# Bucketed attention and a SiLU MLP: another order of Silu and combinations in the last batch's rounds, other buffers for its larger chunk's outputs

## The chip, the cores and the metric

The kernel runs on one core of a Trainium2 chip. Times are device microseconds of one execution, from the median of three runs; the profile is one execution recorded by the hardware profiler, and its span (297.0 us) is a little shorter than the device time of the same run. The engines are named as in the profile: PE multiplies matrices, ACT (ScalarE) evaluates functions and copies, DVE (VectorE) and POOL (GpSimd) do elementwise work, SP issues transfers. Each takes its instructions in a fixed order, and an instruction that waits holds up those behind it.

## The reference, cut to what matters

Four batches of eight heads with 768 tokens and 64 features go through attention in which a query sees only the keys of its own hash bucket (the signs of six projections). The heads of a batch are put side by side into a matrix x of 768 tokens by 512 features, and x goes through two matrices with a SiLU between them:

```
h = x @ w_in                     # (3072 x 512) @ (512 x 2048)
g = h * (1 / (1 + exp(-h)))      # SiLU
out = g @ w_out                  # (3072 x 2048) @ (2048 x 512)
```

The change concerns the second part alone, and of it the last batch.

## The kernel before, in words

For most of the time attention and the MLP run interleaved: while heads of one batch go through attention, the MLP of the batch before fills PE's free places from a list of units. When attention has ended, the last batch's MLP is left, together with some units of the batch before. That is `tail`, from about 248 us of the profile on.

**Seven products instead of eight.** `tail` cuts both matrix products into 2 x 2 blocks and uses the Strassen-Winograd scheme: seven block products (numbered 1 to 7), with sums and differences of blocks before and after. In the first product the two halves of the tokens (384 each) are the rows, so four blocks of h come out: (0,0), (0,1), (1,0) and (1,1), as `gb(r, c, k)` names their SiLU values, k being one of eight blocks of 128 hidden features. `t_comb` forms the differences of x on DVE; those of w_in were made earlier on POOL.

**Rounds.** A loop takes two feature blocks a round: f = 0, 2, 4, 6. For each feature block `prod(n, f)` issues two matmuls of 384 columns (line 689). Products 1, 6, 5 and 3 accumulate one after the other in the same bank of PSUM (`bank[1, f]`, three banks in turn, tag "s"), and after each of the first three ACT copies the running sum out (`copy`, line 699, into `part[1]`, `part[6]`, `part[5]`). So product 6 of a block has to wait for the copy after product 1, product 5 for the copy after product 6, product 3 for the copy after product 5, and product 1 of the block three further on for the Silu that empties the bank. Product 2 has a bank of its own; products 7 and 4 share one (three banks in turn for both, tag "m"). DVE adds these to the copied sums (`add`, line 702): product 2 to part 1, product 7 to part 5, product 4 to part 6. Product 4 of a round is done in the next round (`old`).

**Silu.** A block is finished by Silu on ACT (`silu`, line 705): of part 1 for (0,0), straight from the bank after product 3 for (1,0), of part 5 for (1,1), of part 6 for (0,1). The Silus of parts 5 and 6 take two feature blocks in one instruction (128 x 768); the others take one (128 x 384). Part 5 is ready once product 7 is added; part 6 only in the next round. In the kernel before, the Silu of part 5 stands at the end of its round on ACT, and that of part 6 in the next round, after the copies of product 6.

**Combinations.** The second product needs differences of the Silu values: `combs(f)` makes (1,0)+(1,1) and, from it, s2 on DVE (lines 714 and 716) and s3 on POOL (line 718); `comb4(f)` makes s4 on POOL (line 724). They belong to the round before the one in which they are issued, and stand in DVE's queue ahead of that round's sums of product 2.

**Filler.** `filler` issues one unit of the batch before (eight matmuls of 256 columns, and for some a sum and an output transfer, lines 542 to 553). Rounds f = 0, 2 and 4 have one ahead of product 2, round 6 has none there and one at its end.

**The last product.** `last(ci, n, t)` multiplies the Silu values by w_out, again in seven products, in two chunks of the token blocks: chunk 0 has two blocks of 128 tokens (called the larger one here), chunk 1 one. A loop runs them alternately: 1, -1, 6, -2, 2, -6, 5, -5, 7, 3, -3, -7, 4, -4, a minus sign marking the smaller chunk. A product is 8 matmuls of 256 columns for each token block (line 800). Products 1, 2 share a bank, as do 6, 5, 3 and 7, 4, so -4 has to wait until -7 has been read out. Results of 1, 6 and 5 are kept; those of 2, 3, 7 and 4 are outputs. They are written into a buffer `osb` (line 810 on ACT for product 2, line 812 on DVE for the others) and sent by SP (line 819). All eight outputs take turns in three buffers of one pool, `ops`. The pool `thp` holds three buffers of the same size (128 x 512 in 4 bytes); the rounds keep part 1 in them, and after the rounds nobody does.

Order on each engine is the order of the calls in the code; nothing reorders it.

Of the kernel before, what the change touches and what calls it, by code (L numbers as in the profile page):

```python
# [9 lines left out]
F32 = mybir.dt.float32  # L10
# [7 lines left out]
def kernel(  # L18
# [15 lines left out]
    P = 128  # L34
# [20 lines left out]
    thp = ctx.enter_context(tc.tile_pool(name="thp", bufs=3))  # L55
# [112 lines left out]
    NK = NFT // 2  # L168
    NC = DMODEL // 2
# [286 lines left out]
    def flush():  # L456
        for fn in after:
            fn()
        after.clear()
# [189 lines left out]
    def tail(fill):  # L649
# [16 lines left out]
        def gb(r, c, k, n=1):  # L666
            t = G[2 * (2 * r + c) + k // 4]
            return t[:, k % 4 * NR0 : (k % 4 + n) * NR0]
# [5 lines left out]
        bank, part = {}, {}  # L674

        def prod(n, f):
            i = {1: 1, 6: 1, 5: 1, 3: 1, 2: 2, 7: 3, 4: 3}[n]
            first = n in (1, 2, 7)
            if first:
                bank[i, f] = ps.tile([P, NR0], F32, tag="s" if i == 1 else "m", name="h_ps", bufs=3)  # L680
            for dt in range(2):
                fs = slice(f * P, (f + 1) * P)
                f2 = slice(NF + f * P, NF + (f + 1) * P)
                w, x = {1: (w_in16[:, dt, fs], xb(0, r0, dt)),
                        2: (w_in16[:, 2 + dt, fs], xb(1, r0, dt)),
                        4: (w_in16[:, 2 + dt, f2], T[4][:, dt]),
                        3: (sw[4, dt][:, fs], xb(1, r1, dt))}.get(n) or \
                    (sw[{5: 1, 6: 2, 7: 3}[n], dt][:, fs], T[{5: 1, 6: 2, 7: 3}[n]][:, dt])
                nc.tensor.matmul(bank[i, f], w, x, start=(first and dt == 0), stop=True,  # L689
                                 skip_group_check=True)  # L690

        def copy(n, f):
            if n == 1:
                part[1, f] = thp.tile([P, NR0], F32, tag="th", name="part1")
            elif f % 2 == 0:
                t = ld.tile([P, 2, NR0], F32, tag="ldq" if n == 6 else "ldk", name=f"part{n}")
                part[n, f], part[n, f + 1] = t[:, 0], t[:, 1]
                part[n, "both", f] = t
            nc.scalar.copy(out=part[n, f], in_=bank[1, f])  # L699

        def add(n, i, f):
            nc.vector.tensor_tensor(out=part[n, f], in0=bank[i, f], in1=part[n, f], op=ALU.add)

        def silu(dst, x):
            nc.scalar.activation(out=dst, in_=x, func=AF.Silu)  # L705

        def both(n, f):
            return part[n, "both", f].rearrange("p f c -> p (f c)")

        def combs(f):  # L710
            w = slice(f, f + 2)
            f16 = lambda t: t[:, w].rearrange("p f c -> p (f c)")
            s3[f // 2] = xpl.tile([P, 2 * NR0], F16, tag="xpr", name="gs3", bufs=4)
            nc.vector.tensor_tensor(out=gb(1, 0, f, 2), in0=gb(1, 0, f, 2), in1=gb(1, 1, f, 2),
                                    op=ALU.add)
            nc.vector.tensor_tensor(out=f16(s2), in0=gb(1, 0, f, 2), in1=gb(0, 0, f, 2),
                                    op=ALU.subtract)
            nc.gpsimd.tensor_tensor(out=s3[f // 2], in0=gb(1, 1, f, 2), in1=f16(s2),  # L718
                                    op=ALU.subtract)

        def comb4(f):
            w = slice(f, f + 2)
            f16 = lambda t: t[:, w].rearrange("p f c -> p (f c)")
            nc.gpsimd.tensor_tensor(out=f16(s4), in0=gb(0, 1, f, 2), in1=f16(s2),
                                    op=ALU.subtract)

        def filler(n=1):
            for _ in range(n):
                if fill:
                    fill.popleft()()  # L730
                    flush()

        def old(a):
            for f in (a, a + 1):
                prod(4, f)
                add(6, 3, f)
# [6 lines left out]
        for f in range(0, NK, 2):  # L743
            fs = (f, f + 1)
            for g in fs:
                prod(1, g)
                copy(1, g)
            if f == 0:
                filler(2)
            else:  # L750
                old(f - 2)
            for g in fs:
                prod(6, g)
                copy(6, g)
            if f:
                silu(gb(0, 1, f - 2, 2), both(6, f - 2))
                combs(f - 2)
                comb4(f - 2)
            if f < NK - 2:
                filler()  # L760
            for g in fs:
                prod(2, g)
                add(1, 2, g)
            for g in fs:
                prod(5, g)
                copy(5, g)
            for g in fs:
                prod(7, g)
                add(5, 3, g)
                silu(gb(0, 0, g), part[1, g])  # L770
            for g in fs:
                prod(3, g)
                silu(gb(1, 0, g), bank[1, g])
            silu(gb(1, 1, f, 2), both(5, f))
            if f in (0, NK - 2):
                filler()
        old(NK - 2)
        filler(len(fill))
        combs(NK - 2)
# [5 lines left out]
        def last(ci, n, t):  # L785

            nt, t0 = ((2, 0), (1, 2))[ci]
            i, x, y = {1: (1, (0, 0), B11), 2: (1, (0, 1), B21),
                       6: (2, 2, wt[2]), 5: (2, (1, 0), wt[1]), 3: (2, 4, B22),
                       7: (3, 3, B12), 4: (3, (1, 1), wt[4])}[n]  # L790
            first = t == 0 and n in (1, 6, 7)
            if first:
                bank["o", ci, i] = ps.tile([P, nt, NC], F32, tag="ms"[ci], name="o2_ps", bufs=3)
            op = bank["o", ci, i]
            cs = slice((t0 + t) * P, (t0 + t + 1) * P)
            for k in range(NK):
                a = {2: s2[:, k], 4: s4[:, k],
                     3: s3[k // 2][:, k % 2 * NR0 : (k % 2 + 1) * NR0]}[x] \
                    if isinstance(x, int) else gb(x[0], x[1], k)
                nc.tensor.matmul(op[:, t, :], a[:, cs], y[:, k],  # L800
                                 start=(first and k == 0), stop=True, skip_group_check=True)
            if t < nt - 1:
                return
            with_part = {1: None, 2: None, 6: 1, 5: 1, 3: 1, 7: 5, 4: 6}[n]
            keep = n in (1, 6, 5)
            pool = nrm if keep else ops
            o = pool.tile([P, nt, NC], F32, tag=f"part{ci}{n}" if keep else "osb", name="osb",
                          bufs=1 if keep else 3)
            if with_part is None:
                nc.scalar.copy(out=o, in_=op)  # L810
            else:
                nc.vector.tensor_tensor(out=o, in0=op, in1=kept[ci, with_part], op=ALU.add)
            if keep:
                kept[ci, n] = o
                return
            r, c = {2: (0, 0), 3: (0, 1), 7: (1, 1), 4: (1, 0)}[n]
            dst = out[b * S : (b + 1) * S, c * NC : (c + 1) * NC].rearrange(
                "(p t) n -> p t n", p=P)
            nc.sync.dma_start(out=dst[:, 3 * r + t0 : 3 * r + t0 + nt, :], in_=o)

        for n in (1, -1, 6, -2, 2, -6, 5, -5, 7, 3, -3, -7, 4, -4):
            for t in range(2 if n > 0 else 1):
                last(int(n < 0), abs(n), t)
# [112 lines left out]
    for w in range(NW):  # L936
# [8 lines left out]
        keep = 3 if w >= NW - 12 else 0  # L945
        left = BST - w % BST
        n = -(-(len(moeq) - keep) // left) if len(moeq) > keep else 0
# [5 lines left out]
        if n == 1 and len(moeq) - keep < left and skip:  # L953
            n = 0
# [13 lines left out]
    act = nrm.tile([P, 1], F32, tag="act", name="act", bufs=1)  # L968
    nc.scalar.activation(out=act, in_=sc[:, 0:1], func=AF.Silu)
    tail(late)  # L970
# [1 line left out]
_INS = ['q', 'k', 'v', 'proj', 'moe_w_in', 'moe_w_out']  # L972
# [26 lines left out]
```

The softmax here doesn't subtract the row's maximum and nothing guards it: scores larger than these inputs give would overflow.

## Time and profile before

Time before: 298.57 us, the median of three runs from 298.52 to 298.67. Granted clock of PE in the profile: 1.00.

| | PE | ACT | DVE | POOL |
|---|---|---|---|---|
| busy, whole span of 297.0 us | 288.7 us (97%) | 224.6 us (76%) | 200.5 us (68%) | 202.9 us (68%) |
| busy, 255.64 to 261.12 us (round f = 2) | 5.48 | 4.66 | 4.44 | 2.02 |
| busy, 261.12 to 267.48 us (round f = 4) | 5.80 | 5.54 | 4.49 | 3.74 |
| busy, 267.48 to 273.83 us (round f = 6) | 5.80 | 6.16 | 4.32 | 3.22 |
| busy, 273.83 to 290.20 us (last product) | 16.37 | 3.78 | 6.42 | 3.98 |

The stretches are cut where product 1 of a round starts on PE. An engine's busy time counts only its own instructions, not waits. Matmuls are pipelined and their ends modelled, so a matmul's recorded end lies after the next one's start; a PE stretch without idle time is busy for its whole length. Where a view gives an idle time with "<-", the name behind it is what ended the wait.

### The profile page before, as it was taken

What the parts mean: (1) busy time and instruction counts of PE and PEld (TensorE: products, weight loads), DVE (VectorE), ACT (ScalarE), POOL (GpSimd) and SP (SyncE); (2) the same over time, 40 slices, a digit from 0 to 9 for tenths busy, and PEclk for the clock granted to TensorE, in tenths of its full rate; (3) what the DMA queues carried; (4) which work ended last, traced back from release to release, by engine and by line L of the source; (5) the groups of instructions that cost most, each with busy time, mean ns of one, the idle gap of its engine ahead of it and who ended that gap; (6) DMA issues with size and microseconds to landing.
All of it is one profiled execution on the core that took longest, in us unless ns stands there. A gap on an engine that the chain in (4) does not pass through costs nothing.

```text
span 297.0 us, 7707 instructions
## 1 busy us (share of the span) xinstructions
PE 288.7 (97%) x2918; PEld 196.5 (66%) x2918; DVE 200.5 (68%) x391; ACT 224.6 (76%) x432; POOL 202.9 (68%) x240
## 2 busy tenths in 40 slices
PE   8999999999998999999999999999999999999994
PEld 3666755555666655567666888656668788655883
DVE  5787938898887464855798446964557658776332
ACT  5887998998987676877887786878888863789300
POOL 8588999279997845899357991589998940165400
PEclk9999999999999999999999999999999999999999
DMA  6999999979979439892188425202020212110123
GB/s 206 203 204 246 234 145 139 181 170 155 196 116 205 87 56 189 189 162 55 42 186 122 63 65 153 90 20 51 21 47 2 62 29 88 39 35 3 35 72 124
DMA packets 105877, 33.31 MB, mean 112 GB/s; under 512 B 90800, under 2 KB 105200, under 8 KB 105840
## 3 DMA queue, kind: packets, MB, share of 16 engines
q1 hardware_dynamic: 101456, 28.62, 47.4%
q0 software_dynamic: 4224, 4.19, 9.1%
q8 instruction: 23, 0.38, 0.6%
q14 instruction: 14, 0.11, 0.1%
q10 hardware_dynamic: 160, 0.00, 0.0%
HBM read 27.27 MB, written 6.29 MB: 113 GB/s over the span
## 4 chain that ended last, share of the span: by engine, by line
PE 91%; ACT 3%; DVE 2%; DMA 1%; issue 1%; POOL 0%; ACTq 0%; DVEq 0%; POOLq 0%
PE h_ps L480 21%; PE s_ps L383 20%; PE o_ps L532 14%; PE o_ps L415 12%; PE h_ps L689 5%; PE o_ps L800 4%; PE o_ps L562 4%; PE bp_ps L297 3%; PE tp_ps L201 2%; DMA out_dram<-osb 1%; ACT u L386 1%; PE warm_ps L125 1%; PE bp_ps L241 1%; ACT part L699 1%; ACT th L490 1%
## 5 line engine op out<-in xcount | busy, mean ns | idle before, releaser
L386 ACT ACTIVATE u<-s_ps 128x512 f16<-128x512 f32 x288 | 157.0, 610 | 29.8 <-PE s_ps L383 29.1
L415 PEld LDWEIGHTS <-u 128*128 128x128 f16 x1152 | 67.0, 98 | 37.8 <-ACT u L386 9.3
L415 PE MATMUL o_ps<-vv,u 128*128 128x65 f16 x1152 | 82.5, 194 | 0.6 <-ACT u L386 0.4
L480 PE MATMUL h_ps<-xT,win 128*128 128x512 f16 (+1 forms) x384 | 75.1, 326 | 0.0
L493 DVE SCALAR_TENSOR_TENSOR g<-th,h_ps 128x512 f16<-128x512 f32 x72 | 48.5, 681 | 37.5 <-ACT th L490 37.0
L383 PE MATMUL s_ps<-qka 128*128 128x512 f16 x192 | 52.5, 326 | 0.8 <-DVE osb L566 0.4
L383 PE MATMUL s_ps<-qkb 128*128 128x512 f16 x192 | 53.0, 326 | 0.2 <-ACT u L386 0.2
L490 ACT ACTIVATE th<-h_ps 128x512 f32<-128x512 f32 x72 | 43.8, 608 | 11.0 <-PE h_ps L480 7.6
L480 PEld LDWEIGHTS <-win 128*128 128x128 f16 x384 | 37.5, 98 | 18.0 <-issue 0.4
L532 PEld LDWEIGHTS <-g 128*128 128x128 f16 x336 | 32.8, 98 | 6.8 <-issue 0.3
L435 POOL TENSOR_TENSOR x_pr<-osum,rec 128x384 f16<-128x384 f32 x23 | 19.7, 857 | 25.0 <-DVE rec L434 24.1
L267 POOL TENSOR_SCALAR qka<-qk 64x1536 f16<-64x1536 f32 x15 | 21.9, 1463 | 17.1 <-DVE qk L262 8.4
L267 POOL TENSOR_SCALAR qkb<-qk 64x1536 f16<-64x1536 f32 x15 | 22.0, 1468 | 1.2
L532 PE MATMUL o_ps<-wt,g 128*128 128x256 f16 x168 | 21.6, 272 | 0.1
L532 PE MATMUL o_ps<-wout,g 128*128 128x256 f16 x168 | 21.4, 272 | 0.0
L278 POOL TENSOR_TENSOR vsa<-v_sb 128x192 f32<-128x192 f32 x32 | 18.9, 590 | 0.0
L718 POOL TENSOR_TENSOR gs<-qka,gs 128x768 f16<-128x768 f16 x2 | 3.3, 1642 | 20.7 <-ACT qka L705 18.1
L276 POOL CAST vv<-v_sb 128x384 f16<-128x384 f32 x32 | 16.7, 521 | 0.6
L562 PE MATMUL o_ps<-wout,g 128*128 128x512 f16 x64 | 16.4, 379 | 0.6 <-ACT u L386 0.5
L544 DVE SCALAR_TENSOR_TENSOR osb<-o_ps,osb 128x256 f32<-128x256 f32 (+1 forms) x25 | 13.1, 526 | 4.7 <-PE o_ps L532 4.7
L262 DVE STREAM_TRANSPOSE qk<-k_blk 128x768 f32<-128x768 f32 x10 | 15.9, 1593 | 0.0
L383 PEld LDWEIGHTS <-qka 128*128 128x128 f16 x192 | 15.4, 97 | 0.8 <-ACT qka L254 0.6
(121 smaller groups left out, 440.2 us busy)
## 6 DMA issues: line engine op xcount, KB each, us to landing
v_sb<-in_v_dram SPq DMA_DIRECT2D x15, 384.0 KB
out_dram<-osb SPq DMA_DIRECT2D x16, 256.0 KB
q_blk<-in_q_dram SPq DMA_DIRECT2D x40, 96.0 KB
k_blk<-in_k_dram SPq DMA_DIRECT2D x40, 96.0 KB
win<-in_moe_w_in_dram POOLq DMA_DIRECT2D x4, 512.0 KB, 7.3
wout<-in_moe_w_out_dram POOLq DMA_DIRECT2D x4, 512.0 KB, 6.7
out_dram<-osb SPq DMA_DIRECT2D x16, 128.0 KB
q_sb<-in_q_dram SPq DMA_DIRECT2D x5, 384.0 KB
```

Of the source, the lines that this page charges most:

```text
L267: nc.gpsimd.tensor_scalar(out=dst[rows, :], in0=qk32[p][rows, :], scalar1=CS, scalar2=1.0, op0=ALU.mult, op1=ALU.mult)
L276: nc.gpsimd.tensor_copy(out=vv[:, :, 0:D], in_=src)
L278: nc.gpsimd.tensor_tensor(out=sa, in0=src[:, 0:3], in1=src[:, 3:6], op=ALU.add)
L383: nc.tensor.matmul(sp[:, o0 : o0 + n], t[:, S + jt * P : S + (jt + 1) * P], t[:, c0 : c0 + n], start=True, stop=True)
L386: nc.scalar.activation(out=u, in_=sp, func=AF.Exp, scale=ESC)
L415: nc.tensor.matmul(o_ps[h][:, c0 // P + i, :], u[:, o0 + i * P : o0 + (i + 1) * P], vv[:, jt, :], start=(not direct(h) and w % NU == 0 and ...
L435: (nc.vector if direct(h) else nc.gpsimd).tensor_tensor(out=x_pr[p][:, :, par * D : (par + 1) * D], in0=o[:, 0:NJ, 0:D], in1=rec[:, :, Non ...
L480: nc.tensor.matmul(hp[:, :, j, :], w_in16[:, dt, ft * P : (ft + 1) * P], xT[4 * b + dt][:, c0 : c0 + n] .rearrange("d (r c) -> d r c", r=2 ...
L490: nc.scalar.activation(out=th, in_=hp, func=AF.Tanh, scale=0.5)
L493: nc.vector.scalar_tensor_tensor(out=g, in0=th.rearrange("p r f c -> p r (f c)"), scalar=1.0, in1=hp.rearrange("p r f c -> p r (f c)"), op ...
L532: nc.tensor.matmul(op[:, t, :], x[:, k, t * P : (t + 1) * P], y[:, k], start=(first and k == 0), stop=True, skip_group_check=True)
L562: nc.tensor.matmul(op, x, w_out16[:, ft, :], start=(ft == 0), stop=(ft == NFT - 1))
```

## The change

Three things are moved; no instruction is added or removed. First, ACT's Silu of part 5 leaves the end of its round and goes into the next round, behind the copies of product 6 and ahead of the Silu of part 6 (after the last round it stands at once behind the loop). This is so that the copies of product 1, for which product 6 waits, follow the round's last small Silu directly. Second, the combinations of a round, which need that Silu, go behind the sums of product 2 on DVE. Third, the four outputs of the larger chunk take their buffers from the pool `thp`, so that each chunk has three buffers for its four outputs.

```diff
                 prod(6, g)
                 copy(6, g)
             if f:
+                silu(gb(1, 1, f - 2, 2), both(5, f - 2))
                 silu(gb(0, 1, f - 2, 2), both(6, f - 2))
-                combs(f - 2)
-                comb4(f - 2)
             if f < NK - 2:
                 filler()
             for g in fs:
                 prod(2, g)
                 add(1, 2, g)
+            if f:
+                combs(f - 2)
+                comb4(f - 2)
             for g in fs:
                 prod(5, g)
                 copy(5, g)
...
                 silu(gb(1, 0, g), bank[1, g])
-            silu(gb(1, 1, f, 2), both(5, f))
             if f in (0, NK - 2):
                 filler()
+        silu(gb(1, 1, NK - 2, 2), both(5, NK - 2))
         old(NK - 2)
...
             keep = n in (1, 6, 5)
             pool = nrm if keep else ops
-            o = pool.tile([P, nt, NC], F32, tag=f"part{ci}{n}" if keep else "osb", name="osb",
-                          bufs=1 if keep else 3)
+            if not keep and ci == 0:
+                pool = thp
+            o = pool.tile([P, nt, NC], F32, tag=f"part{ci}{n}" if keep else ("th", "osb")[ci],
+                          name="osb", bufs=1 if keep else 3)
```

## The prediction, on record before the result

> **What bounds the kernel now.** I read the page first, then the chain of waits and the timeline of the tail (from 248 us on), the only stage that the diff touches. On the page PE is busy 97% of the span and holds 91% of the chain that ended last, so the end moves by what PE waits for in the tail, and by what follows PE's last matmul. The chain of the tail (start, duration, what) leaves PE only here:
>
> ```profile
> 259.70 0.86 ACT part L699 x2
> 260.56 1.80 ACT qka L705 x5
> ...
> 262.75 0.51 ACT part L699
> ...
> 263.30 0.87 PE h_ps L689 x4
> ...
> 268.02 0.69 ACT qkb L705 x2
> ...
> 269.11 0.50 ACT part L699
> ...
> 286.91 0.70 DVE osb L812
> ...
> 287.63 4.10 DMA out_dram<-osb
> ...
> 291.85 0.43 DVE osb L812
> ...
> 292.33 1.05 PE o_ps L800 x8
> ```
>
> Two rounds run through ACT, and at the end one DVE instruction waits for a transfer. The timeline (start, duration, engine, ..., idle before and its releaser) of the round f = 4 shows how:
>
> ```profile
> 261.12 0.49 PE L689 MATMUL h_ps<-xT,win 128*128 128x384 f16 x2
> 261.28 0.87 ACT L705 ACTIVATE qka<-h_ps 128x384 f16<-128x384 f32 x2
> 261.82 0.48 PE L689 MATMUL h_ps<-xT,win 128*128 128x384 f16 x2 [0.21 <-ACT qka L705]
> ...
> 262.02 0.86 ACT L705 ACTIVATE qka<-part 128x768 f16<-128x768 f32 x1
> 262.14 0.81 PE L689 MATMUL h_ps<-tx,win 128*128 128x384 f16 x4
> ...
> 262.75 0.88 ACT L699 COPY part<-h_ps 128x384 f32<-128x384 f32 x2
> 263.30 0.87 PE L689 MATMUL h_ps<-tx,sw 128*128 128x384 f16 x4 [0.34 <-ACT part L699]
> ```
>
> Matmul ends are modelled and overlap the next start, so I count from start to start. Four 384-wide matmuls take 0.65 us in flow (0.325 a product). The second product 1 comes at 261.82, 0.70 after the first: 0.37 waiting for the bank that the first L705 of 261.28 empties. Product 6 comes at 263.30, 1.16 after 262.14: 0.51 waiting for the copy of 262.75, which stands behind the Silu of 262.02 (product 5 of the round before). The second copy adds 0.05. That is 0.93 us in this round, and again in f = 6; in f = 2 only 0.05. Rounds start at 255.64, 261.12 and 267.48: 5.48 without waits, 6.36 with them. At the end:
>
> ```profile
> 289.58 0.42 DVE L812 TENSOR_TENSOR osb<-o_ps,osb 128x256 f32<-128x256 f32 x1 [0.18 <-PE o_ps L800]
> ...
> 290.20 0.60 PE L800 MATMUL o_ps<-wt,qka 128*128 128x256 f16 x4
> ...
> 291.85 1.25 DVE L812 TENSOR_TENSOR osb<-o_ps,osb 128x256 f32<-128x256 f32 x2 [1.84 <-DMA out_dram<-osb]
> 292.33 0.60 PE L800 MATMUL o_ps<-wt,qka 128*128 128x256 f16 x4 [0.22 <-DVE osb L812]
> ...
> 293.40 0.42 DVE L812 TENSOR_TENSOR osb<-o_ps,osb 128x256 f32<-128x256 f32 x1 [0.29 <-PE o_ps L800]
> ```
>
> The small chunk's product 7 was ready when PE went on at 290.20, but its sum needs the third output buffer, free only when the transfer issued at 287.63 has landed. PE waits with it, for the bank: 16 matmuls of 0.109 from 290.20 end at 291.95, the next starts at 292.33, 0.38 late.
>
> **What the Trainium skill says.** "ScalarE: Activation LUTs", section "What ACT_TABLE_LOAD costs", prices an ACTIVATE with immediate operands at 186 ns + 0.833 ns an element, and lets neighbours overlap by about 93 ns: estimated 733 ns start to start for 768 elements. The trace agrees (262.02 to 262.75). "Perfetto Trace Analysis", section "Per-instruction lifecycle: what the profiler-reported window actually captures", puts a semaphore wait into the engine's own queue, ahead of execution: what stands behind a waiting or long instruction is late too. The two stalls above are this. "DMA: Bandwidth & Descriptors", section "Anatomy of one DMA — SWDGE (gpsimd) path", gives about 2.0 us + bytes/436 GB/s, an estimated 2.6 us for 256 KB; that is for GpSimd's path, and the 4.10 us here are longer. The trace decides.
>
> **Part 1: Silu of product 5 moved one round on, behind the copies of product 6.** Nothing is added or removed. ACT's order after the last Silu of a round becomes copies 1, copies 6, Silu 5, Silu 6, copies 5, Silu of part 1, Silu of the bank. I lay this out with durations of the trace: copy to copy 0.38, copy to Silu 0.375, big Silu to big Silu 0.735, Silu to copy 0.745, two copies 5 to the first small Silu 0.745, two small Silus 0.84, the bank's Silu 0.49 to its end, 0.05 to PE, and 0.52 from a product's start on PE to its copy.
>
> Round f = 2: product 6 is at 256.95, copies 6 at 257.47, Silu 5 at 258.22, Silu 6 at 258.96, copies 5 at 259.70. Before they started at 259.70 too, then held by PE (which had a filler of 0.87 us to do). The second big Silu thus fits exactly into ACT's idle 0.63 us, and the bank's first Silu ends at 261.77 as before.
> Round f = 4: the second product 1 stays at 261.82. The first copy 1 follows the bank's second Silu (261.65 + 0.37) at 262.02 instead of 262.75; product 6 no longer waits for it and runs at 261.82 + 0.325 + 0.65 = 262.80, 0.50 earlier. Copies 6 at 263.32, Silus at 264.08 and 264.81, copies 5 at 265.56, the bank's Silu from 267.14 to 267.63: the second product 1 of f = 6 at 267.68 instead of 268.18. Gain of the round: 0.50, not 0.93, as the wait for the bank stays (now 0.43).
> Round f = 6: product 6 at 267.68 + 0.975 = 268.65 instead of 269.65, so 1.00 is gained. But this round has no filler ahead of product 2. Copies 6 at 269.17, Silus at 269.93 and 270.67, copies 5 at 271.41, the first done at 271.88. PE, at product 3 at 268.65 + 8 x 0.325 = 271.25, now waits for it until 271.93: 0.68 of new wait. The second product 3 follows its own copy (done at 272.26) at 272.31; before it was at 272.63. Of 1.00 there remain 0.32.
> Bounds: each 0.05 us that ACT needs more between copies 6 and copies 5 counts in three rounds, as the order then has no slack; 0.05 either way gives 0.17 to 0.47.
>
> **Part 2: combinations behind the first sums (DVE, GpSimd).** The same instructions; the two DVE combinations take 0.65 + 0.48 = 1.12 from start to start. The sums of product 2 come that much earlier, those of product 5 later: in f = 2 from 260.42 to about 261.08, read by ACT and PE only from 262.14 on. In f = 6, Silu 5 ends near 270.79 and the combination starts there, not held. GpSimd's two of 1.64 end near 275.3 at the latest before the last combinations (from 275.0); if these wait that out, the last difference is ready near 276.4, and PE reads it at 277.10 - 0.32 = 276.78. All hidden: 0.
>
> **Part 3: the large chunk's four outputs in the other pool's three buffers.** Now four outputs of each chunk share three buffers of their own; only each chunk's fourth reuses one, that of its first output, whose copy is at 281.67 or 279.92 and whose transfer is long over at 291. The wait of product 7 goes, and no new one comes. PE gains 0.38 ahead of the last eight matmuls. The large chunk's last sum, queued behind that of product 7, could start 0.04 after its matmuls (292.11), at 292.15 instead of 292.41: 0.26. Its 256 KB and the final 128 KB leave one after the other, so the end gains between 0.26 (limited by the first) and 0.38; I take 0.30.
>
> **Sum.** 0.32 + 0 + 0.30 = 0.62; 298.57 - 0.62 = 297.95.
>
> **Rivals.**
> A: The Silu pair is slower than laid out by some 0.1 us a round, and the last round gives everything back: part 1 gains 0, part 3 0.26: 298.3. For it: copies 5 have no slack. Against: every interval but Silu to Silu is read off this trace.
> B: The last round doesn't wait anew, for PE reaches product 3 later than I think or ACT is quicker there: 1.00 + 0.30 gained, 297.27. For it: the wait is only 0.68. Against: before, the second copy 5 was already only just in time for product 3 (done near 272.53, product at 272.63), and it now has another 0.74 us of Silu ahead.
> C: Slower. The combinations hold DVE so long that the sums of product 5 keep the banks of products 4 and 7, or Silu 5 keeps the DVE queue: say 0.5 us in each of three rounds, less 0.30: 298.57 + 1.2 = 299.8. Against: product 4 reads its bank 0.4 us or more after these sums in every round laid out; the second product 7 needs only the earlier sum of product 2.
>
> **How the numbers follow.** Forecast 0.66, A 0.19, B 0.08, C 0.07. The forecast is the likeliest. Its own spread, 0.17 + 0.26 to 0.47 + 0.38, is 297.72 to 298.14; to leave out no more than 2 in 10 I reach to A's side and half-way to B: 297.5 to 298.4. The bound of 0.2% is 0.60 us, so the forecast lies on it: about two thirds of it count as faster, one third as same. Faster 0.66 x 0.66 + 0.08 = 0.52; same 0.66 x 0.34 + 0.19 = 0.41; slower 0.07.
>
> **What would show it.** Right: PE's wait for the copies L699 ahead of product 6 is gone in f = 4 and 6; the one for L705 at the second product 1 stays near 0.4 from start to start; a new wait for L699, near 0.7, stands ahead of the last round's product 3; the two later rounds begin about 5.85 us apart; the first output matmul starts near 274.16; no DVE sum waits for an output transfer. Wrong: copies 5 later than 259.75 in f = 2 (A), no new wait (B), PE waiting for DVE in the rounds (C), or the last transfer ending earlier or later than its issue explains.

## The result, and the profile after

The changed kernel takes 297.59 us (median of 6 runs, 297.26 to 297.96) against 298.44 us for the kernel before, measured beside it (6 runs, 297.69 to 298.67). The ratio is 0.9975 with a 95% interval of 0.9962 to 0.9987: faster by 0.75 us, or by 0.39 to 1.13 us at the ends of the interval. The forecast was 0.62 us faster, 297.95 us.

The runs of one kernel scatter by about 1 us, more than the effect. Much of that lies ahead of the tail, in code that the change doesn't touch: the first product 1 of the tail starts at 248.25 us in the first profile of the kernel before and at 247.53 us in that of the changed one. So I cut the tail into two stretches that don't depend on when it begins: **the rounds**, from the first matmul of line 689 to the first output matmul, and **the end**, from there to the end of the span.

| | start of the rounds | rounds | end | span |
|---|---|---|---|---|
| before, first profile | 248.25 | 26.23 | 22.52 | 297.0 |
| changed, first profile | 247.53 | 25.89 | 22.32 | 295.7 |
| before, second profile | 247.27 | 26.24 | 22.30 | 295.8 |
| changed, second profile | 247.62 | 25.89 | 22.31 | 295.8 |

The rounds repeat to 0.01 us in each pair, so 0.35 us of gain there is firm. The end gives 0.20 us in the first pair and nothing in the second.

The timeline of PE in the changed kernel's rounds f = 4 and f = 6 (start, duration, engine, line, operation, tiles, count, and in brackets the idle time before it and what ended it):

```profile
260.34 0.49 PE L689 MATMUL h_ps<-xT,win 128*128 128x384 f16 x2
261.09 0.48 PE L689 MATMUL h_ps<-xT,win 128*128 128x384 f16 x2 [0.26 <-ACT qka L705]
261.41 0.81 PE L689 MATMUL h_ps<-tx,win 128*128 128x384 f16 x4
262.06 0.81 PE L689 MATMUL h_ps<-tx,sw 128*128 128x384 f16 x4
...
269.21 1.46 PE L689 MATMUL h_ps<-tx,sw 128*128 128x384 f16 x8
271.19 0.86 PE L689 MATMUL h_ps<-xT,sw 128*128 128x384 f16 x4 [0.52 <-ACT part L699]
```

The wait for the bank at the second product 1 is still there (261.09 - 260.34 - 0.325 = 0.42 from start to start). Product 6 at 262.06 follows product 4 at once: its wait for copies is gone. A new wait stands before product 3 of the last round: 271.19 - 269.21 - 8 x 0.1625 = 0.68 (0.1625 is one matmul of 384 columns from start to start). The same kernel's timeline of ACT in the last round shows why:

```profile
268.43 0.86 ACT L699 COPY part<-h_ps 128x384 f32<-128x384 f32 x2 [0.42 <-PE h_ps L689]
269.18 1.59 ACT L705 ACTIVATE qkb<-part 128x768 f16<-128x768 f32 x2
270.66 0.86 ACT L699 COPY part<-h_ps 128x384 f32<-128x384 f32 x2
```

From the copies of product 6 on ACT has no idle time, and the two big Silus hold the copies of product 5 until 270.66. PE waits for the first of these.

At the end, DVE's output sums in the changed kernel:

```profile
288.46 0.42 DVE L816 TENSOR_TENSOR osb<-o_ps,osb 128x256 f32<-128x256 f32 x1 [0.18 <-PE o_ps L802]
289.33 0.42 DVE L816 TENSOR_TENSOR osb<-o_ps,osb 128x256 f32<-128x256 f32 x1 [0.45 <-PE o_ps L802]
291.13 1.24 DVE L816 TENSOR_TENSOR osb<-o_ps,osb 128x512 f32<-128x512 f32 x2 [1.38 <-PE o_ps L802]
```

All three are released by PE; the small chunk's product 7 (289.33) waits for no transfer any more. The same view of the second profile of the kernel before, with the old buffers:

```profile
288.61 0.42 DVE L812 TENSOR_TENSOR osb<-o_ps,osb 128x256 f32<-128x256 f32 x1 [0.18 <-PE o_ps L800]
289.43 0.42 DVE L812 TENSOR_TENSOR osb<-o_ps,osb 128x256 f32<-128x256 f32 x1 [0.39 <-PE o_ps L800]
291.21 1.26 DVE L812 TENSOR_TENSOR osb<-o_ps,osb 128x512 f32<-128x512 f32 x2 [1.36 <-PE o_ps L800]
```

Here the old kernel doesn't wait for a transfer either. A wait like the 1.84 us of its first profile comes in some executions and not in others.

### The profile page after: what moved, and what is told of

Same layout as the page of the kernel before. It is cut to its first block, busy times and chain, and to the rows that moved or that the text cites. A ratio compares the mean times of both kernels' runs of the same rounds, so it can differ in the third digit from the quotient of the medians.

```text
span 295.7 us, 7703 instructions
## 1 busy us (share of the span) xinstructions
PE 287.5 (97%) x2918; PEld 196.4 (66%) x2918; DVE 200.9 (68%) x391; ACT 224.5 (76%) x432; POOL 203.0 (69%) x240
## 4 chain that ended last, share of the span: by engine, by line
PE 90%; ACT 5%; DVE 2%; issue 1%; POOL 0%; ACTq 0%; POOLq 0%
PE h_ps L480 21%; PE s_ps L383 20%; PE o_ps L532 14%; PE o_ps L415 12%; PE o_ps L802 6%; PE o_ps L562 4%; PE bp_ps L297 4%; PE h_ps L689 3%; PE tp_ps L201 2%; ACT qka L705 1%; ACT u L386 1%; PE warm_ps L125 1%; ACT part L699 1%; ACT qkb L705 1%; DVE part L702 1%
```

## The experiments

Times are compared with the kernel before, on the same chip. A ratio below 1 is faster, and the range behind it is its 95% interval. Where no ratio is given, the stretches of one execution are read, since single times scatter by about 1 us.

### The output buffers alone

```diff
# against the kernel before
+            if not keep and ci == 0:
+                pool = thp
-            o = pool.tile(..., tag=f"part{ci}{n}" if keep else "osb", ...)
+            o = pool.tile(..., tag=f"part{ci}{n}" if keep else ("th", "osb")[ci], ...)
```

> The kernel before with only the larger chunk's output buffers moved (part 3). I read two stretches of the profile: the rounds, from the first product 1 of f = 0 to the first output matmul (26.23 us before, 25.89 in the changed kernel), and the end, from the first output matmul to the end of the span (22.52 and 22.32). Theory (the two effects are independent and add): rounds 26.23 as before, end about 22.3, so 0.2 faster than before; no sum on DVE waits for an output transfer. Rival (the early rounds moved the end out of the way of something, and the buffers alone give nothing): end 22.5.

Measured: rounds 26.25, end 22.32, no wait for a transfer. The ratio is 0.9995, from 0.9986 to 1.0005, so a gain of 0.15 us is not distinguished from none. The stretches are as the theory has them, but they are compared with the first profile of the kernel before, whose end was the late one. As the second profile of the kernel before ends at 22.30 too, the end of 22.32 here doesn't decide between the theory and its rival.

### The rounds alone

```diff
# against the changed kernel: the output buffers as before
-            if not keep and ci == 0:
-                pool = thp
-            o = pool.tile(..., tag=f"part{ci}{n}" if keep else ("th", "osb")[ci], ...)
+            o = pool.tile(..., tag=f"part{ci}{n}" if keep else "osb", ...)
```

> The changed kernel with its outputs back in the old three buffers (parts 1 and 2 alone). Theory: rounds 25.89 as in the changed kernel, end 22.5 as before, with the small chunk's product 7 again waiting for a transfer and PE 0.38 late; 0.35 faster than before. Rival (all of the gain is at the end or outside the tail): rounds 26.2.

Measured: rounds 25.89, as expected; ratio 0.9984, from 0.9975 to 0.9993, so 0.48 us faster. The end missed the theory: 22.30 and not 22.5, although the wait is there. DVE's timeline:

```profile
290.57 1.11 DVE L814 TENSOR_TENSOR osb<-o_ps,osb 128x256 f32<-128x256 f32 x2 [1.72 <-DMA out_dram<-osb]
292.12 0.42 DVE L814 TENSOR_TENSOR osb<-o_ps,osb 128x256 f32<-128x256 f32 x1 [0.44 <-PE o_ps L802]
```

The transfer released the sum at 290.57, which is 17.25 after the first output matmul; in the first profile of the kernel before it was 17.37. PE's last eight matmuls are 0.26 late here (0.38 there). Yet the larger chunk's last sum starts at 17.67, which is no later than in the changed kernel (17.72).

Why the end doesn't show PE's lateness can be read from the last two transfers, the larger chunk's 256 KB and the final 128 KB behind them (us after the first output matmul):

| | 256 KB issued | final 128 KB issued | last packet ends |
|---|---|---|---|
| before, first profile | 18.65 | 19.37 | 20.83 |
| changed, first profile | 18.44 | 18.99 | 20.62 |
| the rounds alone | 18.39 | 19.25 | 20.62 |
| another order of the last products (below) | 17.57 | 18.99 | 20.36 |

In the first two rows the last packet ends 2.18 after the issue of the 256 KB: the final transfer queues behind them. In the fourth row nothing is left to queue behind, and the last packet ends 1.37 after the final issue. In the kernel with the rounds alone it is 1.37 too (and 2.23 after the 256 KB), so here the final transfer, which PE's lateness delayed, sets the end. The lateness of 0.26 is as long as the queueing that it replaces (20.62 - 20.36), and so the end is the same. PE's lateness is hidden up to about that length. In the first profile of the kernel before, the later 256 KB set the end; with them on time, PE's 0.38 would still have cost 0.12 (an estimate: 19.37 + 1.37 against 20.62).

### The Silu without the combinations

```diff
# against the changed kernel
                 silu(gb(0, 1, f - 2, 2), both(6, f - 2))
+                combs(f - 2)
+                comb4(f - 2)
...
-            if f:
-                combs(f - 2)
-                comb4(f - 2)
             for g in fs:
                 prod(5, g)
```

> The changed kernel with the combinations put back ahead of the sums of product 2, the Silu of part 5 still in the next round. Theory (the combinations had to move with the Silu): DVE waits for that Silu with the sums of product 2 behind it, and the second product 7 waits for these sums to free its bank: about 1.1 us of PE wait in f = 2 and 4 and 1.6 in f = 6; the wait for the bank at product 1 shrinks to 0.13; rounds 28.4, so 2.5 slower than the changed kernel. Rival (moving the combinations is only tidiness, other waits absorb it): rounds 25.9 to 26.2.

Measured: rounds 28.16, 2.28 more than the changed kernel (2.5 expected); ratio 1.0055, from 1.0041 to 1.0069. Before the second product 7 PE waits 1.09, 1.01 and 1.56 us in the three rounds. The timeline of f = 2:

```profile
258.20 0.56 DVE L714 TENSOR_TENSOR qka<-qka,qka 128x768 f16<-128x768 f16 x1 [1.26 <-ACT qka L705]
...
259.68 1.94 DVE L702 TENSOR_TENSOR part<-h_ps,part 128x384 f32<-128x384 f32 x4
...
260.28 0.48 PE L689 MATMUL h_ps<-tx,sw 128*128 128x384 f16 x2 [0.93 <-DVE part L702]
```

The combination waits 1.26 us on DVE for the moved Silu, the sums of product 2 queue behind it until 259.68, and PE waits for their bank. So an instruction that waits holds up those behind it, and the first part of the change needs the second. By itself the second part gains nothing, as the next run shows.

### The combinations without the Silu

```diff
# against the kernel before
                 silu(gb(0, 1, f - 2, 2), both(6, f - 2))
-                combs(f - 2)
-                comb4(f - 2)
...
                 add(1, 2, g)
+            if f:
+                combs(f - 2)
+                comb4(f - 2)
```

> The kernel before with only the combinations moved behind the sums of product 2. Theory (on its own this only delays the sums of product 5, for which the Silu of part 5 at the end of the round waits): that Silu, the copies of product 1 behind it and product 6 come about 0.19 us later in f = 4 and in f = 6: rounds 26.6, 0.4 slower than before. Rival (earlier sums of product 2 help by themselves): rounds 26.2 or less.

Measured: rounds 26.63, 0.40 more than before, as expected; ratio 1.0007, from 0.9998 to 1.0016. The wait for the copies at product 6 is 0.72 and 0.68 in place of 0.51 twice. With the old buffers the end was 22.37. PE was not late, but the larger chunk's last sum was released by a transfer, 17.79 after the first output matmul, 0.09 later than in the second profile of the kernel before.

### The last round's second Silu behind the copies

```diff
# against the changed kernel
                 silu(gb(1, 1, f - 2, 2), both(5, f - 2))
-                silu(gb(0, 1, f - 2, 2), both(6, f - 2))
+                if f < NK - 2:
+                    silu(gb(0, 1, f - 2, 2), both(6, f - 2))
...
                 combs(f - 2)
-                comb4(f - 2)
+                if f < NK - 2:
+                    comb4(f - 2)
             for g in fs:
                 prod(5, g)
                 copy(5, g)
+            if f == NK - 2:
+                silu(gb(0, 1, f - 2, 2), both(6, f - 2))
+                comb4(f - 2)
```

> The changed kernel; in the last round alone the Silu of part 6 (and the GpSimd combination that reads it) goes behind the copies of product 5. Theory (the last round has no filler, so the second big Silu holds up copies 5 and PE waits 0.68 for the first of them): that wait goes, PE goes straight through to the first output matmul; rounds 25.89 - 0.73 = 25.16. The waits of 0.43 at product 1 stay. Rival (ACT is short of time in the last round whatever the order; the delayed Silu makes the output product wait): rounds 25.2 but the first matmuls of product 6 of the output late, or rounds still 25.8.

Measured in one execution: rounds 25.16, end 22.32. PE's timeline of the last round:

```profile
269.47 1.46 PE L689 MATMUL h_ps<-tx,sw 128*128 128x384 f16 x8
270.77 0.81 PE L689 MATMUL h_ps<-xT,sw 128*128 128x384 f16 x4
271.42 1.04 PE L532 MATMUL o_ps<-wt,g 128*128 128x256 f16 x8
```

No gap is left before product 3 (270.77). The new wait was caused by the second big Silu ahead of the copies, not by a shortage of ACT as such.

### Another order of the small Silus

```diff
# against the changed kernel
                 add(5, 3, g)
-                silu(gb(0, 0, g), part[1, g])
             for g in fs:
                 prod(3, g)
+            silu(gb(0, 0, f), part[1, f])
+            for g in fs:
                 silu(gb(1, 0, g), bank[1, g])
+            silu(gb(0, 0, f + 1), part[1, f + 1])
```

> The changed kernel with another order of the small Silus in each round: part 1 of the first block, the two banks, part 1 of the second block. Theory (product 1 waits 0.43 for the bank only because two Silus of part 1 stand ahead of the bank's on ACT): the wait at product 1 falls from 0.43 to about 0.10; copies 1 now come later by one small Silu, so product 6 waits 0.15 + 0.05 in f = 4 and 6, and the last round's wait stays near 0.64; rounds 25.6. Rival (ACT's total work sets the pace of a round, order doesn't matter): rounds 25.9.

Measured in one execution: rounds 25.65. The wait at product 1 fell from 0.42 to 0.09; product 6 waits 0.10 to 0.19 and another 0.06; the last round's wait is 0.62. The gain is 0.23 where 0.29 was expected. The order of the Silus sets this wait.

### Two more copies on ACT

```diff
# against the changed kernel; nobody reads what the copies write
+                nc.scalar.copy(out=warm, in_=ident)
+                nc.scalar.copy(out=dmat, in_=ident)
                 silu(gb(1, 1, f - 2, 2), both(5, f - 2))
                 silu(gb(0, 1, f - 2, 2), both(6, f - 2))
```

> The changed kernel with two copies of 128 x 128 more on ACT in each of the rounds f = 2, 4 and 6, between the copies of product 6 and the Silu of part 5; nobody reads what they write. About 0.19 us start to start each, estimated from the small copies in the trace (0.375 for 384 columns), 0.38 a round. Theory (the order has no slack between copies 6 and copies 5, and each delay counts in three rounds): rounds 25.89 + 3 x 0.38 = 27.0. Rival (there is slack, ACT was idle 0.4 us before copies 6 in each round): rounds 25.9 to 26.3, the last round's alone.

Measured in one execution: rounds 27.08, 1.20 more. ACT's timeline of f = 2:

```profile
257.50 0.31 ACT L756 CAST warm<-ident 128x128 bf16<-128x128 f32 x1
257.69 0.31 ACT L757 CAST dmat<-ident 128x128 bf16<-128x128 f32 x1
257.89 1.58 ACT L705 ACTIVATE qka<-part 128x768 f16<-128x768 f32 x2
259.37 0.86 ACT L699 COPY part<-h_ps 128x384 f32<-128x384 f32 x2
```

The two take 0.39 from start to start, and copies 5 come later by as much. Three times 0.39 is 1.17: every delay between copies 6 and copies 5 counts in full in each of three rounds. ACT's idle 0.4 us ahead of copies 6 doesn't absorb it, since it lies before the point where ACT becomes the one to wait for.

### Another order of the last products

```diff
# against the changed kernel
-        for n in (1, -1, 6, -2, 2, -6, 5, -5, 7, 3, -3, -7, 4, -4):
+        for n in (1, -1, 6, -2, 2, -6, 5, -5, 7, 3, -7, 4, -3, -4):
```

> The changed kernel with another order of the last output products: 7, 3, -7, 4, -3, -4 in place of 7, 3, -3, -7, 4, -4, so that the larger chunk's last 256 KB leave one small product earlier. Theory (the end is set by that transfer's issue, which the final 128 KB follow): the final transfer no longer queues behind it, the end stretch is 22.05 to 22.1 instead of 22.32. Rival (the end is set by the last matmul and a fixed cost of the final transfer): 22.3.

Measured in one execution: rounds 25.89, end 22.05, with the last matmul issued 18.23 after the first output matmul, exactly as in the changed kernel. DVE's last sums:

```profile
290.22 1.24 DVE L816 TENSOR_TENSOR osb<-o_ps,osb 128x512 f32<-128x512 f32 x2 [1.38 <-PE o_ps L802]
291.91 0.42 DVE L816 TENSOR_TENSOR osb<-o_ps,osb 128x256 f32<-128x256 f32 x1 [0.45 <-PE o_ps L802]
```

The larger chunk's last sum comes 16.85 after the first output matmul in place of 17.72, the final sum at 18.54 as in the changed kernel. So 0.26 of the end belonged to the queue behind the 256 KB, as the theory says.

### The three orders together, and both kernels again

The next kernel takes the last round's late Silu, the order of the small Silus and the order of the last products together, with the diffs above. Then follow the changed kernel and the kernel before once more.

> The three orders that each shortened a stretch, together, on top of the changed kernel: the late Silu of part 6 in the last round (-0.73), banks before the second Silu of part 1 (-0.23), the larger chunk's product 4 ahead of the smaller one's product 3 (-0.26). Theory (three separate waits, so they add): rounds 24.9, end 22.05, 1.2 us below the changed kernel, near 1.8 us below the kernel before. Rival (the rounds' two gains share the last round and overlap): rounds 25.15, 0.25 less in all.

Measured: 296.55 us (median of 6) against 298.23, a ratio of 0.9941, from 0.9918 to 0.9964. Rounds 24.97, end 22.04: 1.19 below the changed kernel. The three add, and this version is faster than both kernels.

> The changed kernel itself, for a second profile and more times beside the kernel before. Theory (the tail gives 0.35 in the rounds and 0 to 0.2 at the end, the rest of the first measured difference is scatter of the executions ahead of the tail): 0.35 to 0.55 us faster in the median, rounds 25.89 and end 22.3 again, the start of the rounds between 247.2 and 248.3. Rival (the change also speeds up what comes before the tail): 0.8 us or more faster.

Measured: 297.69 us (median of 22) against 298.23, a ratio of 0.9980, from 0.9972 to 0.9988, so 0.60 us faster, or 0.36 to 0.83. Rounds 25.89, end 22.31, start 247.62. The interval excludes neither the theory (0.35 to 0.55) nor, by a little, the rival (0.8 or more); the starts, here and in the next run, give the rival no support.

> The kernel before itself, for a second profile. Theory (its stretches repeat but for where an instruction fetch falls among the last transfers): rounds 26.23, end between 22.3 and 22.5, start of the rounds earlier than the 248.25 of its first profile. Rival (the first profile is typical, the kernel before reaches its tail later than the changed one): start again near 248.2.

Measured in one execution: rounds 26.24, end 22.30, start 247.27. The kernel before can start its rounds earlier than the changed one (the output buffers alone and the combinations alone, with the same code ahead of the tail, start at 247.18 and 247.19). So the first pair's difference ahead of the tail was scatter.

## Why the prediction was right, point by point

**What bounds the tail.** Right. With PE's waits and the last transfers alone, each of the runs above could be told in advance to 0.1 us in its stretches, but for two: the end of the kernel with the rounds alone (0.2 off), and the rounds of the Silu without the combinations (28.16 for 28.4). All of these expectations were written with the first pair's stretches known.

**Part 1, 0.32.** Right in mechanism and size: 0.35 in both pairs of profiles. Counted from the rounds' start, product 6 of f = 4 came 0.52 earlier (forecast 0.50), the second product 1 kept a wait of 0.42 (forecast 0.43), and the new wait of the last round was 0.68 (forecast 0.68). Taking away that wait (rounds 25.16) and adding work to ACT (three times the added time) show that the layout's claims hold: the last round gives back 0.68 of the 1.02 that product 6 had gained by then, and ACT has no slack between the copies. Rival A's condition, no slack, is true; its slower Silu pair isn't: from the first copy 6 to the first copy 5 of f = 2 it took 2.23 (256.74 to 258.97), as laid out (257.47 to 259.70). Rival B (no new wait) is what one more edit makes of the kernel. A wait of PE for DVE, which rival C fears, comes only when the combinations don't move along, and then behind the sums of product 2, not of product 5.

**Part 2, 0.** Right in its sum. The case that it allowed for came true: the last combination had to wait for GpSimd, as told below, and this stayed hidden.

**Part 3, 0.30.** The mechanism was right and the term too large: in the first pair the end fell by 0.20, in the second by nothing. That the new buffers take the wait away is shown. In the first profile of the changed kernel the transfer of product 7 took as long to land as before (4.17 us from its issue, before 4.10), and nobody waited for it; in none of the nine profiles with the new buffers does a sum wait for a transfer.

Two things made the term too large. First, the wait is not in every execution. With the old buffers the sum of the small chunk's product 7 waited in two profiles, and PE was late (0.38 and 0.26); in a third only the larger chunk's last sum waited, and in the fourth none. I had read one profile's wait as the kernel's. Second, less of it reaches the end. The larger chunk's last sum moved from 17.93 to 17.72 after the first output matmul, 0.21 in place of 0.26, since it started 0.09 after the modelled end of its matmuls (291.04 to 291.13) and not 0.04. The upper figure, PE's 0.38, was out of reach: with the 256 KB ahead of the final transfer, about 0.26 of such lateness is hidden. By these profiles, the new buffers are worth 0 to 0.2 us.

**The sum.** 0.62 forecast; the stretches give 0.35 + 0 to 0.20, and the two timings 0.75 (0.39 to 1.13) and 0.60 (0.36 to 0.83). The parts timed alone add to 0.48 + 0.15 = 0.63. That these come so near to 0.62 is in part luck: one of the two terms was too large, and both timings lie above what the tail's stretches give, though their intervals reach down to it. The profiles don't explain the rest. The difference between the first pair's 1.3 us in the spans and its 0.55 us in the tail lies ahead of the tail, and did not come back in the second pair.

## What to carry to other kernels

Where one engine's queue feeds another in a loop, lay out both queues with durations from the trace and carry each delay round the loop: taking an instruction out of one wait puts it ahead of another, and the round that lacks filler work pays. A wait of a microsecond for a transfer in one profile may be absent in the next, so take a second profile before counting it. At the end of a kernel, look at which transfer is issued last but one: a large one just ahead of the last can set the end, and then an earlier last matmul gains nothing.

## What the runs showed of the hardware

**DVE's 16-bit combination waits for GpSimd.** The last combination of the changed kernel took 0.88 us; alone it takes 0.55. DVE's timeline, and below it that of GpSimd:

```profile
273.30 1.01 DVE L702 TENSOR_TENSOR part<-h_ps,part 128x384 f32<-128x384 f32 x2
274.23 0.88 DVE L714 TENSOR_TENSOR qkb<-qkb,qkb 128x768 f16<-128x768 f16 x1
```

```profile
273.05 1.64 POOL L724 TENSOR_TENSOR gs<-qkb,gs 128x768 f16<-128x768 f16 x1
```

GpSimd's difference runs until 274.69, and the combination ends 0.42 after that. In the kernel with the combinations alone the overlap was longer (1.19 us) and the combination took 1.61, again to 0.42 after GpSimd's end. The sums at 273.30, with one input in PSUM, ran at their usual length beside the same GpSimd instruction. The Trainium skill, "SBUF — State Buffer", section "SBUF: two separate sides", says that a DVE operation with two SBUF inputs and a GpSimd operation that reads SBUF share one pair of ports as an exclusive lock, and that the one that comes second blocks; the runs agree. Here the last difference was still ready at 275.71, before PE reached product 6 at 276.03.

**A transfer that is held up by an instruction fetch, perhaps.** In the first profile of the kernel before, 251 of the 256 packets of product 7's transfer left in one burst of 0.85 us, and the last five later, after the next transfer had begun. The trace records the landing of a transfer in 16 parts: 15 of them came within 2.14 us of the issue, the last after 4.10. The instruction queue's row of the transfers between 287.6 and 291.8 us (packets, megabytes, share of 16 engines), and that of the like 4.2 us of the second profile of the kernel before:

```profile
q8 instruction: 1, 0.02, 2.0%
```

```profile
q8 instruction: 1, 0.02, 1.3%
```

One 16 KB fetch took 1.31 us on one of the 16 engines in the first and 0.88 us in the second. In the first it began during the transfer, in the second just after the transfer's last packet; there all 256 packets left in one burst, and nobody waited. The Trainium skill, "Runtime: NRT & Kernel Launch", section "Instruction fetch mechanics", says that engines fetch instructions in blocks of 16 KiB over a DMA queue of their own, and that this is mostly hidden.

All 13 profiles have a fetch at about this place, and in all of them the last of the 16 parts lands after the others; in the transfer of product 2, as large and with no fetch near it, all 16 land within 2.18 us. In nine profiles the last part lands 3.5 to 4.2 us after the issue, and 1.1 to 1.4 us after the fetch's end; in the other four it lands 2.4 to 2.6 us after the issue, before the fetch ends. So a long delay goes with a part that comes only after the fetch. That the fetch is what holds it is inferred from this and not shown, as no run moves the fetch, and in the changed kernel's first profile five packets were late with the fetch recorded as beginning only after the burst. It stays open.
